# A weight half on another queue, a transposing load on ScalarE's queue, and a new order for the first projections

## The chip, the cores and the metric

The kernel runs on one core of one Trainium2 chip. Such a core has five engines that run their own instruction streams: TensorE (PE, the matmuls, with a separate stream of weight loads called PEld in the profile), VectorE (DVE), ScalarE (ACT), GpSimd (POOL) and SyncE (SP). SP does no arithmetic; here it issues DMAs, and ACT issues a few as well. Each engine takes its instructions in the order in which they stand, and an instruction that has to wait holds up everything behind it on the same engine. The engines meet through semaphores: an instruction waits until a counter has reached a value, and DMAs raise such counters when they have landed.

The metric is the device time of one execution in microseconds (us). The kernel before has a median of 178.42 us over three runs (178.19 to 178.46). The profile below is of one further execution that took 178.12 us; its span, from the first to the last instruction, is 176.3 us, so 1.8 us lie around the span.

## The reference

The input `x` has 2048 tokens of 512 numbers in bf16. Two branches are computed from it and mixed token by token with a gate:

```
g = sigmoid((x * gate_w).sum(-1))
# A: linear attention, 32 heads of 16
q, k, v = split(x @ wqkv)
phi(t)  = where(t > 0, t + 1, exp(t)) + 1e-6
kv = phi(k)^T v   per head;   z = sum over tokens of phi(k)
a  = (phi(q) kv) / (phi(q) . z + 1e-6)  @ wo
# B: a gated feed-forward block with F = 1376
b  = (silu(x @ w1) * (x @ w3)) @ w2
out = g * a + (1 - g) * b
```

## The kernel before, in words

The tokens lie in 16 tiles of 128, and four tiles make one of four blocks of 512. The width 512 is cut into `KC` = 4 chunks of 128, so that one projection of a tile (128 tokens by 512 columns) is four matmuls that add up in one PSUM buffer, one for each chunk `kc`.

**What the projections read.** `k` of tile t (`emit_k_mm`, line 195) takes as its stationary side the transposed tokens `xT[:, kc, tile t]` and as its moving side `wk_sb[:, kc, :]`. So chunk `kc` of tile t needs the transposed tile t and chunk `kc` of `wk`. `wk_sb` comes in two halves: chunks 0 and 1 (line 84) and chunks 2 and 3 (line 85), both issued by ACT.

**How `xT` is filled.** Tile 0 is loaded plainly into `x_sb` (line 83) and transposed on TensorE by `emit_xT(0)` (lines 180 to 192), whose two copies out of PSUM run on DVE (chunks 0 and 1) and ACT (chunks 2 and 3). All other tiles come by DMAs that transpose on their way: tile 1 and then tiles 2 and 3 in one load of 256 tokens (lines 88 and 89), and then blocks 1, 2 and 3 with 512 tokens each (line 92). Between these stand the plain loads of `x_sb` (line 97). After them come `wq`, the remainder columns `wr`, `wv`, `w1`, `w3`, `wo` and `w2` (lines 98 to 112). All of it stands on SP's queue in that order; before the change no transposing load stands on another queue.

**The beginning on TensorE.** `emit_warm` (line 163) first runs matmuls over constants into a PSUM buffer that nobody reads: 20 that use 32 columns of the array each (line 168), one of 128 by 128 (line 172), then come the four transposes of tile 0, three more warm matmuls, and the four `k` projections of block 0 in the order of the tiles, each with its four chunks (lines 418 to 421). After each projection `emit_k_phi` applies phi (line 145 Exp on ACT, lines 147 and 150 on DVE) and adds the result into `pks` on POOL (lines 203 and 205). From tile 4 on, `k` projections alternate with `emit_xp(u)` (line 215), which multiplies `x_sb` of a tile with phi(k) of the same tile; it needs phi of tile u. The order on TensorE is the order of the source, since PE is under a manual schedule throughout; ACT and DVE are ordered by a scheduler except where a `manual_schedule` names them.

**The later stages.** After the 16 `k` projections come `q` of block 0, the remainder columns, the small product `kvT` (lines 463 to 470), the first gate projection `gate0`, of which `emit_gate_tiled` (line 326) runs 16 matmuls that use 32 columns each, the product `W_ps` (line 487), and then the feed-forward block with the outputs, block by block.

The semaphore waits are placed by the framework that builds the program; the source does not name them.

Of the kernel before, what the change touches and what calls it, by code (L numbers as in the profile page):

```python
# [11 lines left out]
ENG = mybir.EngineType  # L12
# [5 lines left out]
def kernel(  # L18
# [12 lines left out]
    nc = tc.nc  # L31
    P = nc.NUM_PARTITIONS

    Bb, S, D = A_x.shape
# [3 lines left out]
    KC = D // P  # L38
    NT = S // P
    TB = 512  # L40
    NTB = S // TB
    TPB = TB // P
    FC = F // P
    FR = F - FC * P
    FM = FC * P
    NR = 2 * FR + 1
# [5 lines left out]
    x2d = A_x.flatten_outer_dims()  # L52
# [13 lines left out]
    xT = consts.tile([P, KC, S], BF16, name="xT")  # L66
    wk_sb = consts.tile([P, KC, D], BF16, name="wk_sb")
# [4 lines left out]
    wr_sb = consts.tile([P, KC, 2 * P], BF16, name="wr_sb")  # L72
# [4 lines left out]
    wqkv_r = A_wqkv.rearrange("(kc d) n -> d kc n", d=P)  # L77
# [2 lines left out]
    x_r = x2d.rearrange("(t p) d -> p t d", p=P)  # L80
    dq = nc.sync
    TF = 1
    dq.dma_start(out=x_sb[:, 0, :], in_=x2d[0:P, :])
    nc.scalar.dma_start(out=wk_sb[:, 0:2, :], in_=wqkv_r[:, 0:2, D : 2 * D])  # L84
    nc.scalar.dma_start(out=wk_sb[:, 2:4, :], in_=wqkv_r[:, 2:4, D : 2 * D])
    pre = consts.tile([1, 1], FP32, name="pre")
    nc.scalar.activation(out=pre[:], in_=nc.const_aps.tensor(0.0, [1, 1], FP32), func=ACT.Exp)
    for tsl in (slice(P, 2 * P), slice(2 * P, TB)):
        dq.dma_start(out=xT[:, :, tsl], in_=x2d[tsl, :], transpose=True)
    x_cut = [TF, TPB + 2, 3 * TPB, NT]  # L90
    for tb in range(1, NTB):
        dq.dma_start(
            out=xT[:, :, tb * TB : (tb + 1) * TB], in_=x2d[tb * TB : (tb + 1) * TB, :],
            transpose=True,
# [4 lines left out]
    dq.dma_start(out=wr_sb[:, :, 0:FR], in_=w1_r[:, :, FM:F])  # L99
    dq.dma_start(out=wr_sb[:, :, FR : 2 * FR], in_=w3_r[:, :, FM:F])  # L100
    with nc.allow_non_contiguous_dma(reason="one gate weight per partition and chunk"):
        dq.dma_start(
            out=wr_sb[:, :, 2 * FR : NR], in_=gate_w.rearrange("(kc d o) -> d kc o", d=P, o=1)
        )
    dq.dma_start(out=wv_sb[:], in_=wqkv_r[:, :, 2 * D : 3 * D])
    dq.dma_start(out=w1_sb[:], in_=w1_r[:, :, 0:FM])
    for fsl in (slice(0, FM // 2), slice(FM // 2, FM)):
# [12 lines left out]
        out=bm, in_=bm, pattern=[[-Dh, HPC], [0, Dh]], compare_op=ALU.is_ge, fill=0.0,  # L120
# [3 lines left out]
        out=bm, in_=bm, pattern=[[Dh, HPC], [0, Dh]], compare_op=ALU.is_ge, fill=0.0,  # L124
# [18 lines left out]
    def phi(dst, ps):  # L143
        e = work.tile([P, D], BF16, tag="phi_e", name="phi_e")
        e_ins = nc.scalar.activation(out=e[:], in_=ps, func=ACT.Exp)  # L145
        em = work.tile([P, D], BF16, tag="phi_m", name="phi_m")
        nc.vector.tensor_scalar(  # L147
            out=em[:], in0=e[:], scalar1=1.0, scalar2=1e-6, op0=ALU.min, op1=ALU.add
        )
        nc.vector.scalar_tensor_tensor(  # L150
            out=dst, in0=ps, scalar=0.0, in1=em[:], op0=ALU.max, op1=ALU.add
        )
        return e_ins
# [9 lines left out]
    def emit_warm(tiled, whole, tag="XP3"):  # L163
        warm = psX.tile([P, TB], FP32, tag=tag, name="warm")
        for n in tiled:
            for i in range(NG):
                gsl = slice(i * G, (i + 1) * G)
                nc.tensor.matmul(
                    warm[gsl, 0:n], lhsT=warm_l[:, gsl], rhs=warm_r[:, 0:n], start=True, stop=True
                )  # L170
        for n in whole:
            nc.tensor.matmul(
                warm[:, 0:n], lhsT=warm_l, rhs=warm_r[:, 0:n], start=True, stop=True
            )

    emit_warm((TB, TB, TB, TB, TB), (P,))

    st = {}

    def emit_xT(t):  # L180
        for h in range(2):
            xTp = psX.tile([P, 2, P], BF16, tag=f"XP{(2 * t + h) % 4}", name="xTp")
            for j in range(2):
                kc = 2 * h + j
                nc.tensor.transpose(
                    out=xTp[:, j, :], in_=x_sb[:, t, kc * P : (kc + 1) * P], identity=ident[:]
                )
            xT_t = xT[:, 2 * h : 2 * h + 2, t * P : (t + 1) * P]
            if h == 0:
                nc.vector.tensor_copy(out=xT_t, in_=xTp[:])  # L190
            else:
                nc.scalar.activation(out=xT_t, in_=xTp[:], func=ACT.Copy)

    def emit_k_mm(k_ps, t, kc):
        nc.tensor.matmul(  # L195
            k_ps[:], lhsT=xT[:, kc, t * P : (t + 1) * P], rhs=wk_sb[:, kc, :],
            start=(kc == 0), stop=(kc == KC - 1),
        )

    def emit_k_phi(k_ps, t):  # L200
        e_ins = phi(pk_sb[:, t, :], k_ps[:])
        if t == 0:
            nc.gpsimd.tensor_copy(pks[:], pk_sb[:, t, :])
        else:
            nc.gpsimd.tensor_add(pks[:], pks[:], pk_sb[:, t, :])  # L205
# [117 lines left out]
            )  # L323
        st[tb, "pqT"] = pqT

    def emit_gate_tiled(gate_ps):
        for kc in range(KC):
            for i in range(NG):
                gsl = slice(i * G, (i + 1) * G)
                nc.tensor.matmul(  # L330
                    gate_ps[gsl, :], lhsT=w1_sb[:, kc, gsl], rhs=xT[:, kc, 0:TB],
                    start=(kc == 0), stop=(kc == KC - 1),
                )
# [79 lines left out]


    k0 = [psM.tile([P, D], FP32, tag="mm", name=f"k0_{t}") for t in range(TPB)]
    emit_xT(0)
    emit_warm((), (P, P, P))
    for t in range(TPB):
        for kc in range(KC):
            emit_k_mm(k0[t], t, kc)  # L420
        emit_k_phi(k0[t], t)

# [11 lines left out]
    with tc.manual_schedule(engines={ENG.DVE}):  # L434
        Q = 32
        NB = D // Q
        zt = consts.tile([P, NB, Q], FP32, name="zt")
        nc.vector.transpose(out=zt[:].rearrange("p b f -> p (b f)"), in_=pks[:])
        w = Q // 2
        while w >= 1:  # L440
            nc.gpsimd.tensor_add(zt[:, :, 0:w], zt[:, :, 0:w], zt[:, :, w : 2 * w])
            w //= 2
        zq = zt[:, :, 0]
        z_up = consts.tile([P // 2, NB], FP32, name="z_up")
        z_h = consts.tile([P // 2, NB], FP32, name="z_h")
        z_hi = consts.tile([Q, NB], FP32, name="z_hi")
        z_col = consts.tile([P, NB], FP32, name="z_col")
        nc.gpsimd.tensor_copy(z_up[:], zq[P // 2 : P, :])
        nc.gpsimd.tensor_add(z_h[:], zq[0 : P // 2, :], z_up[:])
        nc.gpsimd.tensor_copy(z_hi[:], z_h[Q : 2 * Q, :])  # L450
        for b in range(P // Q):
            nc.gpsimd.tensor_add(z_col[b * Q : (b + 1) * Q, :], z_h[0:Q, :], z_hi[:])
        for dc in range(KC):
            if dc % 2 == 0:
                nc.scalar.activation(out=XP_sb[:, dc, :], in_=XP_ps[dc][:], func=ACT.Copy)
            else:
                nc.vector.tensor_copy(out=XP_sb[:, dc, :], in_=XP_ps[dc][:])

        emit_q(0, TPB - 1, psM, "mm")
        rem0 = [emit_rem_mm(0, half, psM, "mm") for half in range(2)]  # L460
        kvT_ps = psX.tile([P, KC, G], FP32, tag="XP0", name="kvT_ps")
        gate0 = psM.tile([P, TB], FP32, tag="mm", name="gate0")
        for c in range(KC):
            for dc in range(KC):
                for i in range(NG):
                    bsl = slice(c * P + i * G, c * P + (i + 1) * G)
                    nc.tensor.matmul(  # L467
                        kvT_ps[i * G : (i + 1) * G, c, :], lhsT=wv_sb[:, dc, bsl],
                        rhs=XP_sb[:, dc, bsl], start=(dc == 0), stop=(dc == KC - 1),
                    )  # L470
        nc.vector.tensor_tensor(
            out=kvT_sb[:], in0=kvT_ps[:],
            in1=diagmask[:, None, :].to_broadcast([P, KC, G]), op=ALU.mult,
        )
        for half in range(2):
            emit_rem_h(0, half, *rem0[half])
        nc.vector.transpose(
            out=z_sb[:].rearrange("p (b f) -> p b f", f=Q),
            in_=z_col[:, :, None].to_broadcast([P, NB, Q]),
        )  # L480

        emit_gate_tiled(gate0)
        W_ps = [psX.tile([P, D], FP32, tag=f"XP{i}", name=f"W_ps{i}") for i in range(NG)]
        for i in range(NG):
            gsl = slice(i * G, (i + 1) * G)
            for c in range(KC):
                nc.tensor.matmul(  # L487
                    W_ps[i][c * G : (c + 1) * G, :], lhsT=kvT_sb[gsl, c, :],
                    rhs=wo_sb[gsl, c, :], start=True, stop=True,
                )  # L490

        emit_omg(0)
        emit_ffn(0, 0, gate=gate0)
# [72 lines left out]
```

## Time and profile before

| what | us |
|---|---|
| median of three runs | 178.42 |
| the profiled execution | 178.12 |
| its span | 176.3 |
| TensorE busy in the span | 172.7 |
| VectorE busy | 119.9 |
| ScalarE busy | 64.5 |
| GpSimd busy | 66.9 |

The granted TensorE clock is 1.000 over the whole span. In the profile a row of the timeline gives the start and the length in us, the engine, the line, the operation, what is written from what, and how many instructions are merged in the row; in brackets stands how long the engine was idle ahead of it and what ended that. `SPq` and `ACTq` are instructions by which SP and ACT issue DMAs; the time from that issue to the landing of the data stands in the list of DMA issues. `L195` is line 195. The records of successive matmuls overlap, so that the chain of waits, which counts from start to start, is the better measure of the pace.

### The profile page before, as it was taken

What the parts mean: (1) busy time and instruction counts of PE and PEld (TensorE: products, weight loads), DVE (VectorE), ACT (ScalarE), POOL (GpSimd) and SP (SyncE); (2) the same over time, 40 slices, a digit from 0 to 9 for tenths busy, and PEclk for the clock granted to TensorE, in tenths of its full rate; (3) what the DMA queues carried; (4) which work ended last, traced back from release to release, by engine and by line L of the source; (5) the groups of instructions that cost most, each with busy time, mean ns of one, the idle gap of its engine ahead of it and who ended that gap; (6) DMA issues with size and microseconds to landing.
All of it is one profiled execution on the core that took longest, in us unless ns stands there. A gap on an engine that the chain in (4) does not pass through costs nothing.

```text
span 176.3 us, 2655 instructions
## 1 busy us (share of the span) xinstructions
PE 172.7 (98%) x966; PEld 82.6 (47%) x966; DVE 119.9 (68%) x204; ACT 64.5 (37%) x121; POOL 66.9 (38%) x100
## 2 busy tenths in 40 slices
PE   8999999999999999999999999999999999999994
PEld 3344444464445454444454544444545444444463
DVE  0588778898999637597875466977854669776000
ACT  4442224475424333324243333233434323331222
POOL 7298555779109423282003232820032329100000
DMA  5999999911002311124000101240002022300002
GB/s 174 236 271 281 262 386 363 348 45 26 9 4 60 67 37 37 37 63 89 0 0 7 58 20 47 59 82 0 6 7 67 7 66 54 66 4 0 30 30 60
DMA packets 30524, 15.27 MB, mean 87 GB/s; under 512 B 21456, under 2 KB 30000, under 8 KB 30512
## 3 DMA queue, kind: packets, MB, share of 16 engines
q1 hardware_dynamic: 29824, 14.54, 30.3%
q10 hardware_dynamic: 688, 0.57, 1.0%
q8 instruction: 7, 0.11, 0.3%
q14 instruction: 5, 0.04, 0.1%
HBM read 8.42 MB, written 2.10 MB: 60 GB/s over the span
## 4 chain that ended last, share of the span: by engine, by line
PE 96%; DMA 2%; ACTq 0%; DVE 0%; issue 0%
PE up_ps L353 20%; PE o_ps L395 20%; PE gate_ps L345 19%; PE o_ps L386 8%; PE q_ps L228 8%; PE XP L215 8%; PE k_ps L195 6%; PE r_ps L251 3%; DMA wk_sb<-in_A_wqkv_dram 2%; PE o_ps L390 2%; PE k L195 2%; PE gate L330 0%; PE kvT_ps L467 0%; ACTq L84 0%; PE W_ps L487 0%; DVE o_last L404 0%
## 5 line engine op out<-in xcount | busy, mean ns | idle before, releaser
L353 PE MATMUL up_ps<-xT,w_sb 128*128 128x512 bf16 x160 | 41.1, 379 | 0.0
L345 PE MATMUL gate_ps<-xT,w_sb 128*128 128x512 bf16 x156 | 40.0, 379 | 0.0
L236 POOL TENSOR_TENSOR qz<-pq,z_sb 128x512 f32<-128x512 bf16 x16 | 18.5, 1164 | 53.5 <-DVE pq L150 53.5
L358 ACT ACTIVATE th<-gate_ps 128x512 bf16<-128x512 f32 x39 | 23.3, 597 | 39.8 <-PE gate_ps L345 38.3
L395 PE MATMUL o_ps<-w_sb,hT 128*128 128x512 bf16 (+3 forms) x180 | 37.5, 355 | 0.0
L360 DVE SCALAR_TENSOR_TENSOR gs<-th,gate_ps 128x512 bf16<-128x512 bf16 x39 | 26.6, 683 | 5.6 <-ACT th L358 5.3
L365 DVE TENSOR_TENSOR hT<-up_ps,gs 128x512 bf16<-128x512 f32 x40 | 27.5, 690 | 3.7 <-PE gate_ps L345 0.5
L147 DVE TENSOR_SCALAR phi_m<-phi_e 128x512 bf16<-128x512 bf16 x32 | 16.2, 507 | 19.6 <-ACT phi_e L145 19.5
L311 POOL TENSOR_TENSOR pqn<-pq,rden 128x256 bf16<-128x256 bf16 x32 | 19.0, 625 | 16.5 <-DVE rden L302 15.1
L395 PEld LDWEIGHTS <-hT 128*128 128x128 bf16 x180 | 16.9, 98 | 17.8
L353 PEld LDWEIGHTS <-w_sb 128*128 128x128 bf16 x160 | 15.6, 98 | 18.9 <-issue 0.2
L345 PEld LDWEIGHTS <-w_sb 128*128 128x128 bf16 x156 | 15.3, 98 | 18.4
L400 ACT ACTIVATE o_out<-o_ps,omg 128x512 bf16<-128x512 f32 x15 | 10.3, 687 | 28.7 <-PE o_ps L395 28.7
L205 POOL TENSOR_TENSOR pks<-pks,pk_sb 128x512 f32<-128x512 f32 x15 | 17.4, 1158 | 8.1 <-DVE pk_sb L150 7.6
L386 PE MATMUL o_ps<-W_sb,pqT 128*128 128x512 bf16 (+3 forms) x72 | 16.8, 355 | 0.0
L228 PE MATMUL q_ps<-wq_sb,xT 128*128 128x512 bf16 x64 | 16.4, 379 | 0.0
L239 DVE TENSOR_REDUCE den<-qz 128x32 f32<-128x512 f32 x16 | 11.0, 685 | 7.9 <-POOL qz L236 7.8
L215 PE MATMUL XP<-pk_sb,x_sb 128*128 128x512 bf16 x64 | 15.9, 379 | 0.0
L145 ACT ACTIVATE phi_e<-k_ps 128x512 bf16<-128x512 f32 x12 | 7.2, 597 | 14.4 <-PE k_ps L195 10.4
L145 ACT ACTIVATE phi_e<-q_ps 128x512 bf16<-128x512 f32 x16 | 9.6, 597 | 7.8 <-PE q_ps L228 7.8
L195 PE MATMUL k_ps<-wk_sb,xT 128*128 128x512 bf16 x48 | 12.0, 379 | 0.0
L150 DVE SCALAR_TENSOR_TENSOR pq<-q_ps,phi_m 128x512 bf16<-128x512 f32 x16 | 11.1, 691 | 0.5
(68 smaller groups left out, 119.4 us busy)
## 6 DMA issues: line engine op xcount, KB each, us to landing
w_sb<-in_B_w_dram SPq DMA_DIRECT2D x2, 1280.0 KB, 9.7
out_dram<-o_out SPq DMA_DIRECT2D x15, 128.0 KB, 1.7
w_sb<-in_B_w_dram SPq DMA_DIRECT2D x2, 640.0 KB, 8.3
x_sb<-in_A_x_dram SPq DMA_DIRECT2D x1, 768.0 KB, 5.2
x_sb<-in_A_x_dram SPq DMA_DIRECT2D x1, 640.0 KB, 4.4
wk_sb<-in_A_wqkv_dram ACTq DMA_DIRECT2D x2, 256.0 KB, 3.3
x_sb<-in_A_x_dram SPq DMA_DIRECT2D x1, 512.0 KB, 4.8
wq_sb<-in_A_wqkv_dram SPq DMA_DIRECT2D x1, 512.0 KB, 5.7
```

What stands on the lines that cost most here:

```text
L195: nc.tensor.matmul(k_ps[:], lhsT=xT[:, kc, t * P : (t + 1) * P], rhs=wk_sb[:, kc, :], start=(kc == 0), stop=(kc == KC - 1),)
L215: nc.tensor.matmul(XP_ps[dc][:], lhsT=x_sb[:, t, dc * P : (dc + 1) * P], rhs=pk_sb[:, t, :], start=(t == 0), stop=(t == NT - 1),)
L228: nc.tensor.matmul(q_ps[:], lhsT=xT[:, kc, ts_tok], rhs=wq_sb[:, kc, :], start=(kc == 0), stop=(kc == KC - 1),)
L236: nc.gpsimd.tensor_tensor(out=qz[:], in0=st[tb, "pq"][:, tt, :], in1=z_sb[:], op=ALU.mult)
L311: nc.gpsimd.tensor_tensor(out=pqn[:].rearrange("p (i c e) -> p c i e", i=NG, c=KC)[:, :, :, dsl], in0=st[tb, "pq"][:, tt, :].rearrange("p ...
L345: nc.tensor.matmul(gate_ps[:], lhsT=w1_sb[:, kc, fsl], rhs=xT[:, kc, tok_sl], start=(kc == 0), stop=(kc == KC - 1),)
L353: nc.tensor.matmul(up_ps[:], lhsT=w3_sb[:, kc, fsl], rhs=xT[:, kc, tok_sl], start=(kc == 0), stop=(kc == KC - 1),)
L358: nc.scalar.activation(out=th[:], in_=gate_ps[:], func=ACT.Tanh, scale=0.5)
L360: nc.vector.scalar_tensor_tensor(out=gs[:], in0=th[:], scalar=1.0, in1=gate_ps[:], op0=ALU.add, op1=ALU.mult)
L365: nc.vector.tensor_tensor(out=st[tb, "hT"][:, fc, :], in0=up_ps[:], in1=gs[:], op=ALU.mult)
L386: nc.tensor.matmul(o_ps[:], lhsT=st[tb, "pqT"][:, c, tsl], rhs=W_sb[:, c, a:b], start=(c == 0), stop=False,)
L395: nc.tensor.matmul(o_ps[:], lhsT=st[tb, "hT"][:, fc, tsl], rhs=w2_sb[:, fc, a:b], start=False, stop=(fc == FC - 1),)
```

## The change

Five things are done:

- The second half of `wk` is issued by SP, between the transposing load of tile 1 and the next one, instead of by ACT at the beginning.
- The load of tiles 2 and 3 becomes two. Tile 2 stays on SP's queue. Tile 3 is issued by ACT, in a manual schedule of ACT that holds `emit_xT(0)` and this load, so that it stands behind ACT's copy of tile 0's transposes and ahead of phi.
- Tiles 0 and 1 take `wk`'s first half first: the order of (chunk, tile) is (0,0), (1,0), (0,1), (1,1), (2,0), (3,0), then phi of tile 0, then chunks 2 and 3 of tile 1, then tiles 2 and 3 as before.
- One warm matmul of 128 by 128 ahead of the transposes is left out.
- Of the 16 matmuls of `gate0`, the four of chunk 0 move between the second and the third column group of `kvT`.

The naming of `gate_r` ahead of its use changes nothing.

```diff
@@ -80,13 +80,16 @@
     dq = nc.sync
     TF = 1
+    gate_r = gate_w.rearrange("(kc d o) -> d kc o", d=P, o=1)
     dq.dma_start(out=x_sb[:, 0, :], in_=x2d[0:P, :])
     nc.scalar.dma_start(out=wk_sb[:, 0:2, :], in_=wqkv_r[:, 0:2, D : 2 * D])
-    nc.scalar.dma_start(out=wk_sb[:, 2:4, :], in_=wqkv_r[:, 2:4, D : 2 * D])
     pre = consts.tile([1, 1], FP32, name="pre")
     nc.scalar.activation(out=pre[:], in_=nc.const_aps.tensor(0.0, [1, 1], FP32), func=ACT.Exp)
-    for tsl in (slice(P, 2 * P), slice(2 * P, TB)):
+    for t in range(TF, TPB - 1):
+        tsl = slice(t * P, (t + 1) * P)
         dq.dma_start(out=xT[:, :, tsl], in_=x2d[tsl, :], transpose=True)
+        if t == TF:
+            dq.dma_start(out=wk_sb[:, 2:4, :], in_=wqkv_r[:, 2:4, D : 2 * D])
...
@@ -173,7 +174,7 @@
-    emit_warm((TB, TB, TB, TB, TB), (P,))
+    emit_warm((TB, TB, TB, TB, TB), ())
...
-    def emit_gate_tiled(gate_ps):
-        for kc in range(KC):
+    def emit_gate_tiled(gate_ps, lo, hi):
+        for kc in range(lo, hi):
...
@@ -413,10 +414,16 @@
     k0 = [psM.tile([P, D], FP32, tag="mm", name=f"k0_{t}") for t in range(TPB)]
-    emit_xT(0)
+    with tc.manual_schedule(engines={ENG.Activation}):
+        emit_xT(0)
+        t3sl = slice(3 * P, TB)
+        nc.scalar.dma_start(out=xT[:, :, t3sl], in_=x2d[t3sl, :], transpose=True)
     emit_warm((), (P, P, P))
-    for t in range(TPB):
-        for kc in range(KC):
+    for kc, t in ((0, 0), (1, 0), (0, 1), (1, 1), (2, 0), (3, 0)):
+        emit_k_mm(k0[t], t, kc)
+    emit_k_phi(k0[0], 0)
+    for t in range(1, TPB):
+        for kc in range(2 if t == 1 else 0, KC):
             emit_k_mm(k0[t], t, kc)
         emit_k_phi(k0[t], t)
...
@@ -461,6 +468,8 @@
         for c in range(KC):
+            if c == KC // 2:
+                emit_gate_tiled(gate0, 0, 1)
             for dc in range(KC):
...
-        emit_gate_tiled(gate0)
+        emit_gate_tiled(gate0, 1, KC)
```

More of the change, by code (lines that the diff above doesn't have):

```diff
@@ L101 @@
     with nc.allow_non_contiguous_dma(reason="one gate weight per partition and chunk"):
-        dq.dma_start(
-            out=wr_sb[:, :, 2 * FR : NR], in_=gate_w.rearrange("(kc d o) -> d kc o", d=P, o=1)
-        )
+        dq.dma_start(out=wr_sb[:, :, 2 * FR : NR], in_=gate_r)
     dq.dma_start(out=wv_sb[:], in_=wqkv_r[:, :, 2 * D : 3 * D])
```

## The prediction

> **What bounds the kernel now.** I read the page's chain of waits first, then the chain in order of time, then the timeline of the first nine microseconds, and last the list of DMA issues for narrow stretches.
>
> The page's chain of what ended last has one line by engine:
>
> ```profile
> PE 96%; DMA 2%; ACTq 0%; DVE 0%; issue 0%
> ```
>
> TensorE carries the span. In order of time (start, length, what) the beginning reads:
>
> ```profile
> 0.80 0.46 ACTq L84
> 1.26 0.03 issue
> 1.29 3.70 DMA wk_sb<-in_A_wqkv_dram
> 4.99 0.04 issue
> 5.03 3.34 PE k L195 x14
> 8.38 0.86 PE XP L215 x4
> 9.24 2.59 PE k_ps L195 x12
> ```
>
> The reader is to see two things. Up to 5.03 us the chain waits for `wk`'s second half; from there to the last matmul TensorE does not stop. So time can be won only ahead of 5 us, and any new stop of TensorE goes into the time in full. The pace of the full clock is also here: 12 matmuls in 2.59 us, 0.216 us each. The timeline (start, length, engine, line, what) shows how the pieces of the beginning stand:
>
> ```profile
> 0.84 2.33 PE L168 MATMUL warm<-const-bfloat16-1.0 128*32 128x512 bf16 x20 [0.84 <-PEq L550]
> ...
> 1.26 2.62 SPq L89 DMA_TRANSPOSE xT<-in_A_x_dram  x2
> 1.29 0.49 ACTq L85 DMA_DIRECT2D wk_sb<-in_A_wqkv_dram  x1
> ...
> 3.85 0.38 ACT L192 ACTIVATE xT<-xTp 128x256 bf16<-128x256 bf16 x1 [0.54 <-PE xTp L185]
> 3.93 2.17 SPq L92 DMA_TRANSPOSE xT<-in_A_x_dram  x1
> 3.98 0.13 PEld L195 LDWEIGHTS <-xT 128*128 128x128 bf16 x2
> 3.99 0.86 PE L195 MATMUL k<-wk_sb,xT 128*128 128x512 bf16 x2
> ...
> 5.03 3.34 PE L195 MATMUL k<-wk_sb,xT 128*128 128x512 bf16 x14 [0.18 <-DMA wk_sb<-in_A_wqkv_dram]
> ...
> 5.41 0.59 PEld L195 LDWEIGHTS <-xT 128*128 128x128 bf16 x4 [0.28 <-DMA xT<-in_A_x_dram]
> ...
> 6.47 1.41 PEld L195 LDWEIGHTS <-xT 128*128 128x128 bf16 x8 [0.48 <-DMA xT<-in_A_x_dram]
> ...
> 6.77 3.53 SPq L92 DMA_TRANSPOSE xT<-in_A_x_dram  x1
> ```
>
> TensorE waits 0.18 us for `wk`; tile 1 arrives just in time (5.41), and so do tiles 2 and 3 (6.47). The four matmuls of tile 3 are the last of the fourteen; they start 0.86 us ahead of 8.38, at 7.52 us. The list of DMA issues for stretches around one issue gives the time from issue to landing, first around 1.5 us (tile 1), then around 6.7 us (block 2):
>
> ```profile
> xT<-in_A_x_dram SPq DMA_TRANSPOSE x1, 4.1
> ...
> xT<-in_A_x_dram SPq DMA_TRANSPOSE x1, 5.7
> ```
>
> So tile 1 lands at 1.26 + 4.1 = 5.4 us, and block 2 at 6.77 + 5.7 = 12.5 us, five microseconds after TensorE wants tile 3.
>
> **The change part by part.** *Tile 3 on ACT's queue* is the term that decides. In the changed program as it is built, ACT's load of tile 3 stands behind waits for five DMA counters: those of the plain tile 0, of the transposing loads of tile 1, tile 2 and block 1, and of the transposing load of block 2. By these waits the framework keeps the transposing loads of two queues apart; all three block loads stand ahead of tile 3's in the source, and two of them in the built order. SP's load of block 3 in its turn waits for tile 3's counter. TensorE's first weight load of tile 3 waits for that counter too. Nothing of this exists before.
>
> When ACT is released: SP issues, in the new order, tile 0, tile 1, `wk`'s half (0.49, its row on ACT), tile 2 (1.28; the merged row of two is 2.62 for 128 and 256 tokens, so the size hardly matters here), block 1, the plain five tiles, block 2. Against before one plain issue is added, 0.49 and a gap of 0.04: block 2 is issued at 6.77 + 0.53 = 7.30 and lands, with the same 5.7, at 13.0. It could be earlier, since 128 KB less stand ahead of it in a stretch that moved 250 to 300 GB/s: 0.5 us off, 12.0 without the later issue. Or later: a plain load now breaks the run of transposes once more. I take 12.9, ends 12.0 and 13.4.
>
> How long tile 3 takes: the nearest row is tile 1's load, the same 128 tokens from the same tensor beside 640 KB of plain loads: 4.1. At 13 us it runs beside the plain load of six tiles, 768 KB. The transposing loads of `pqT`, equal in size but out of SBUF and with a quiet queue, have a median of 2.4. Block 2 itself, four times the size in a full queue, has 5.7. I take 3.6, nearest to tile 1 and a little shorter since tile 1's also held the start of everything; ends 2.4 and 5.7. Landing: 12.9 + 3.6 = 16.5 us.
>
> TensorE is in order: behind tile 3's weight load stand `XP` of tile 0, `k` of tile 4 and all that follows. It starts tile 3 at 16.5 instead of 7.52: **+9.0 us**.
>
> *The clock after the stop.* The first two `k` matmuls took 0.86 us, 0.43 each, against 0.216 later. TensorE ran at half pace from 0.84 to 4.85 us, 4.0 us of work that would have been 2.0: the ramp costs 2.0 us once. Between tile 2's end (issued at 3.1, 4.0 to its landing as the median of the two loads before, 0.86 of matmuls: 7.9) and 16.5 it stands still for 8.6 us, longer than that whole ramp. The trace of before has no such stop in the middle, so what comes after one is bounded by 0 and by a full second ramp, 2.0. I take **+2.0**, because the only rows that follow idleness are the slow ones.
>
> [...]
>
> *ACT held up.* ACT waits from 4.23 (the end of its copy at 3.85 + 0.38) to 12.9, and behind that wait stand the Exps of tiles 0 to 2, for which DVE, POOL and later `XP` wait. ACT is free again after an issue of 1.28 at 14.2; Exp 0.60, then 0.29 and 0.69 on DVE give phi of tile 0 at about 15.8, ahead of `XP`, which can't start before tile 3's four matmuls, 16.5 plus 0.86 or more. Tiles 1 and 2 follow at about one microsecond each, and free the PSUM buffers for tiles 5 and 6 in time, as TensorE at half pace takes 1.7 us for each group of four. Cost nothing; the cover is TensorE's own late start.
>
> *SP held up.* Block 3's issue moves from 10.97 to 16.5, and all weights behind it by as much, 5.5 us; TensorE's need for each moves by 11. No weight made TensorE wait before, so none does now. Nothing.
>
> *`wk`'s half and the new order.* The half is issued at about 2.6 instead of 1.29 and lands, with 2.2 (tile 0's plain load) to 3.7 (its own row), at 4.8 to 6.3. The first four matmuls need tile 1, which landed at 5.4, and are through by 5.8. So the 0.18 of waiting may go, or become a wait of up to 0.5. TensorE ends in front of tile 3 anyway and waits there for 8 us: in the sum 0.
>
> *The warm matmul left out.* It ran at 3.10, while tile 0 landed at 0.81 + 2.2 = 3.01; tile 0's transposes may start some 0.1 earlier. Also swallowed: 0.
>
> *`gate0`'s four matmuls among `kvT`'s.* The same 16 and 64 matmuls in another order. `kvT`'s last ends a quarter of the gate's 0.88 later, 0.22, and DVE's masked copy (0.29) with it; `W_ps` waits for that copy; in between TensorE now has 12 gate matmuls, three quarters of 0.88, 0.66 us, over 0.29 and DVE's gap of 0.1. Cost 0; with that cover gone 0.3. In the built order one small Exp on ACT falls behind the gate's Tanh (0.58), so DVE's first feed-forward step comes about 0.5 later. Its second product ends at 43.55, and TensorE wants that buffer at 44.46, so 0.9 of slack holds it.
>
> **The sum.** 9.0 + 2.0 = 11.0 us on the profiled 178.12: 189.1. The median stands 0.3 above the profiled execution, so 189.4 us is the forecast.
>
> [...]
>
> **The rivals.**
>
> 1. *The clock does not fall.* Only the stop of 9.0 counts: 187.4 us. Speaks for it: the granted clock in the profile is 1.000 throughout, even in the slow rows, so it does not show this state. Against: those slow rows themselves.
> 2. *Tile 3 lands later still*, as a load beside 768 KB in a full queue: with block 2's 5.7 it lands at 18.6, 11.1 after 7.52, plus 2.0: 191.5 us. For it: landings grow from 4.1 to 5.7 and 8.0 for blocks 2 and 3. Against: those are four times the size.
> 3. *The stop is not there*, the other side: if tile 3 landed by 7.5, TensorE would lose nothing and keep what is won ahead, the 0.18 wait for `wk` and 0.1 of the warm matmul: 178.1 us. It decides at a landing of 7.5, for which ACT would have to be released by 3.9 (3.6 earlier), ahead of the end of its own copy at 4.23. Only if the waits stood for loads that are done early could this be.
> 4. *The stop is short*, because only tiles 1 and 2 need be waited for: ACT released near 7.0, landing at 10.6, a stop of 3.1, shorter than the ramp and taken without one: 181.5 us. Against it stand the counters of blocks 1 and 2.
>
> **How the numbers follow.** I give the forecast 0.64, rival 1 0.13, rival 2 0.17, rival 3 0.03, rival 4 0.03. Within 0.2% of before, which is about what a measurement of this kernel can tell from no change, lies rival 3's 178.1: 0.02 for the same and, as it might win a little more, 0.01 for faster. Slower is the rest, 0.97. The bounds together: 12.0 + 2.4 = 14.4 gives +6.9, with the ramp 187.3, without it 185.3; 13.4 + 5.7 = 19.1 gives +11.6 + 2.0, 192.0. The range takes in most of that, 186.5 to 191.8 us; the low end leaves out rival 1 with the earliest landing, and the two rivals below it.
>
> **What would show it.** In the profile of the changed kernel the wait list of ACT should have a wait of about 8.7 us for the DMA of `xT` at line 420; TensorE should be idle about 8.6 us in one piece before the last four `k` matmuls of block 0, released by `xT`; the matmuls behind it should go at 0.43 each for some 4 us; the last three slices of weights should land without a wait of TensorE; and nothing in the span behind some 21 us should be longer than before. Wrong would be: a stop that ends before 14 us or after 19, matmuls at 0.216 right behind it, or a second wait of TensorE, for phi or for block 3.

## The result, and the profile after

The changed kernel takes 190.91 us (median of six runs, 190.35 to 191.82) against 178.45 us before (six runs, 178.19 to 179.05): 1.070 times as long, 95% interval 1.068 to 1.073. The forecast was 189.4 us with a range of 186.5 to 191.8. The profiled execution took 190.56 us with a span of 188.8 us, 12.5 us more than the span before.

Two lines of the page of the changed kernel, the chain's shares by engine and the granted TensorE clock in 40 slices of the span, in tenths:

```profile
PE 89%; DMA 5%; SPq 3%; issue 1%; DVE 0%; ACTq 0%
...
PEclk9975699999999999999999999999999999999999
```

TensorE's share has fallen from 96% to 89%, that of DMAs has grown from 2% to 5%, and SP's issues have come in with 3%. The page of before has no line for the clock; now there is one, and it has a dip in slices 3 to 5, about 9 to 24 us. The chain of waits in order of time (start, length, what), from 7 us on:

```profile
7.36 6.41 DMA xT<-in_A_x_dram
13.77 0.02 issue
13.79 0.04 ACTq L420
13.82 0.04 issue
13.86 3.39 DMA xT<-in_A_x_dram
17.25 0.05 issue
17.30 1.89 PE k L196 x4
19.19 1.71 PE XP L216 x4
20.89 0.85 PE k_ps L196 x2
21.75 0.21 issue
21.95 2.11 PE k_ps L196 x9
24.06 0.86 PE XP L216 x4
...
185.95 0.28 DVE o_last L405
```

The same chain before has the second group of `XP` and the last eviction here:

```profile
11.83 0.86 PE XP L215 x4
...
173.76 0.28 DVE o_last L404
```

This is the whole story in one column. Block 2's transposing load is issued at 7.36 and lands 6.41 later; that releases line 420 on ACT; tile 3's load takes 3.39; then TensorE starts tile 3 at 17.30. Before, it started tile 3 at 7.52, so it is 9.78 us late. From there to the second group of `XP` it now needs 24.06 - 17.30 = 6.76 us, where it needed 11.83 - 7.52 = 4.31: another 2.45. From 24 us on the two chains run in step: the last matmuls' eviction on DVE starts at 185.95 instead of 173.76, 12.19 later. The remaining 0.3 lie in the final stores.

The timeline (start, length, engine, line, what, and in brackets the idle time ahead and its end) shows who waits:

```profile
6.26 1.89 PE L196 MATMUL k<-wk_sb,xT 128*128 128x512 bf16 x8 [0.77 <-DMA wk_sb<-in_A_wqkv_dram]
...
7.36 4.39 SPq L95 DMA_TRANSPOSE xT<-in_A_x_dram  x1
11.79 0.58 SPq L100 DMA_DIRECT2D x_sb<-in_A_x_dram  x1
13.86 1.27 ACTq L420 DMA_TRANSPOSE xT<-in_A_x_dram  x1
15.18 1.57 ACT L146 ACTIVATE phi_e<-k 128x512 bf16<-128x512 f32 x3 [11.05 <-issue]
...
17.27 2.00 SPq L95 DMA_TRANSPOSE xT<-in_A_x_dram  x1
...
17.30 1.89 PE L196 MATMUL k<-wk_sb,xT 128*128 128x512 bf16 x4 [9.15 <-DMA xT<-in_A_x_dram]
```

ACT computes nothing from 4.13 to 15.18, TensorE nothing for 9.15 us, and SP issues block 3 only at 17.27, when tile 3 has landed. The idle time of the first Exp is put down to "issue" and not to a DMA: the load's own wait for other loads does not show as a wait of ACT in this view; it is seen from the start of the row of line 420.

The windows of the same kernel give, for each stretch, its length, the busy time of PE, PEld, DVE, ACT and POOL, then the granted clock, the share of the DMA engines and their GB/s:

```profile
8.00:12.00 4.00, 0.15 (x1) 0.00 (x0) 0.00 (x0) 0.00 (x0) 0.00 (x0) 0.96 0.98 241
12.00:16.00 4.00, 0.00 (x0) 0.00 (x0) 0.19 (x1) 0.82 (x2) 0.00 (x0) 0.50 0.96 263
16.00:18.00 2.00, 0.70 (x2) 0.28 (x3) 1.90 (x6) 0.76 (x2) 0.70 (x2) 0.50 0.37 85
...
21.00:22.00 1.00, 0.79 (x3) 0.35 (x3) 0.17 (x1) 0.00 (x0) 0.69 (x1) 0.53 0.85 247
22.00:24.00 2.00, 2.00 (x10) 0.93 (x10) 0.97 (x3) 1.19 (x2) 0.47 (x1) 1.00 1.07 353
```

A mean of 0.96 over 8 to 12 us means, with the 1.00 and 0.50 of the stretches on either side, that the clock went from 1.00 to 0.50 at about 11.7, some 3.5 us after TensorE had stopped. It came back at 21.9 (0.53 over 21 to 22), 4.6 us after TensorE had started again.

### The profile page after: what moved, and what is told of

It is laid out like the page before. It is cut to its first block, busy times and chain, and to the rows that moved or that the text cites. A ratio compares the mean times of both kernels' runs of the same rounds, so it can differ in the third digit from the quotient of the medians.

```text
span 188.8 us, 2641 instructions
## 1 busy us (share of the span) xinstructions
PE 174.0 (92%) x949; PEld 83.0 (44%) x965; DVE 118.1 (63%) x204; ACT 64.1 (34%) x121; POOL 66.8 (35%) x100
## 4 chain that ended last, share of the span: by engine, by line
PE 89%; DMA 5%; SPq 3%; issue 1%; DVE 0%; ACTq 0%
PE up_ps L354 18%; PE o_ps L396 18%; PE gate_ps L346 18%; PE XP L216 8%; PE o_ps L387 7%; PE q_ps L229 7%; PE k_ps L196 6%; DMA xT<-in_A_x_dram 5%; PE r_ps L252 3%; PE o_ps L391 2%; SPq L90 1%; SPq L95 1%; PE k L196 1%; PE gate L331 0%; SPq L100 0%
## 5 line engine op out<-in xcount | busy, mean ns | idle before, releaser
L148 DVE TENSOR_SCALAR phi_m<-phi_e 128x512 bf16<-128x512 bf16 x32 | 14.3, 448 | 33.5 <-ACT phi_e L146 33.5
L396 PEld LDWEIGHTS <-hT 128*128 128x128 bf16 x180 | 16.8, 98 | 17.8
L354 PEld LDWEIGHTS <-w_sb 128*128 128x128 bf16 x160 | 15.6, 98 | 18.9 <-issue 0.2
L216 PE MATMUL XP<-pk_sb,x_sb 128*128 128x512 bf16 x62 | 16.6, 395 | 0.1
L196 PEld LDWEIGHTS <-xT 128*128 128x128 bf16 x64 | 6.5, 103 | 19.4 <-DMA xT<-in_A_x_dram 10.4
L196 PE MATMUL k<-wk_sb,xT 128*128 128x512 bf16 x16 | 5.2, 466 | 10.0 <-DMA xT<-in_A_x_dram 9.2
L146 ACT ACTIVATE phi_e<-k_ps 128x512 bf16<-128x512 f32 x12 | 7.2, 597 | 15.8 <-PE k_ps L196 14.7
```

Source lines behind the costliest of these rows:

```text
L196: nc.tensor.matmul(k_ps[:], lhsT=xT[:, kc, t * P : (t + 1) * P], rhs=wk_sb[:, kc, :], start=(kc == 0), stop=(kc == KC - 1),)
L216: nc.tensor.matmul(XP_ps[dc][:], lhsT=x_sb[:, t, dc * P : (dc + 1) * P], rhs=pk_sb[:, t, :], start=(t == 0), stop=(t == NT - 1),)
L354: nc.tensor.matmul(up_ps[:], lhsT=w3_sb[:, kc, fsl], rhs=xT[:, kc, tok_sl], start=(kc == 0), stop=(kc == KC - 1),)
L396: nc.tensor.matmul(o_ps[:], lhsT=st[tb, "hT"][:, fc, tsl], rhs=w2_sb[:, fc, a:b], start=False, stop=(fc == FC - 1),)
```

## The experiments

The theory was: the loss is the wait of ACT's load for block 2's load, and then the second ramp of the clock. Against it stood: that other parts of the change carry a part of the loss, that any load on ACT's queue would do this, and that the slow stretch behind the stop comes from late phi and not from the clock.

**Tile 3 on ACT's queue, and nothing else.** The kernel before with this edit:

```diff
-    for tsl in (slice(P, 2 * P), slice(2 * P, TB)):
+    for tsl in (slice(P, 2 * P), slice(2 * P, 3 * P)):
...
-    emit_xT(0)
+    with tc.manual_schedule(engines={ENG.Activation}):
+        emit_xT(0)
+        t3sl = slice(3 * P, TB)
+        nc.scalar.dma_start(out=xT[:, :, t3sl], in_=x2d[t3sl, :], transpose=True)
```

> The kernel before with one edit: tile 3's transposing load is taken out of the load of tiles 2 and 3 and issued by ScalarE behind its copy of tile 0's transposes; wk, the order of the projections, the warm matmul and the gate stay as before. Theory (ScalarE's load waits for block 2's load, and nothing else in the change matters): block 2 lands at about 12.5 us, tile 3 3.4 later at 15.9, TensorE's last four k matmuls of block 0 start 8.4 later than before, plus 2.4 for the second ramp of the clock: 189.2 us, 188 to 190.5. Rival (the stop needs the later half of wk or the new order): 178.4 to 180 us.

Measured: 189.08 us against 178.65 us, ratio 1.059 (1.055 to 1.064). Two rows of its timeline:

```profile
13.19 1.28 ACTq L419 DMA_TRANSPOSE xT<-in_A_x_dram  x1
...
16.34 1.89 PE L195 MATMUL k<-wk_sb,xT 128*128 128x512 bf16 x4 [8.61 <-DMA xT<-in_A_x_dram]
```

The one edit brings 10.4 of the 12.5 us. Tile 3 is 16.34 - 7.52 = 8.8 us late, and the ramp, measured as above up to the second group of `XP` (at 22.32), is 1.7. The other 2 us of the changed kernel are a start of tile 3 that is 0.96 later (block 2 is issued at 7.36 instead of 6.62, and tile 3's own load takes 3.39 instead of 3.10) and a ramp that is 0.8 longer.

**Tile 3 back on the sync queue, the rest of the change kept.**

```diff
-    for t in range(TF, TPB - 1):
+    for t in range(TF, TPB):
...
-    with tc.manual_schedule(engines={ENG.Activation}):
-        emit_xT(0)
-        t3sl = slice(3 * P, TB)
-        nc.scalar.dma_start(out=xT[:, :, t3sl], in_=x2d[t3sl, :], transpose=True)
+    emit_xT(0)
```

> The changed kernel, but tile 3's transposing load stands on the sync queue right behind tile 2's; the rest of the change stays. Theory (all of the large loss is tile 3 on ScalarE's queue; the rest costs a little since wk's second half lands at 6.2 instead of 5.0 us and each further transposing issue takes 1.28): tile 3 lands at about 8.3, its four matmuls end at about 9.2 instead of 8.4: 179.2 us, 178.7 to 179.8. Rival (the moved half of wk and the new order carry part of the loss): 181 us or more. Second rival (the rest of the change by itself is a gain): 178.2 us or less.

Measured: 179.63 us against 178.41, ratio 1.0065 (1.0045 to 1.0085). What TensorE waits for in it (us in total, times, longest):

```profile
PE k_ps L196 <- DMA xT<-in_A_x_dram: 0.7, 1, 0.7
PE k L196 <- DMA wk_sb<-in_A_wqkv_dram: 0.4, 1, 0.4
PE XP L216 <- DMA x_sb<-in_A_x_dram: 0.3, 1, 0.3
```

So the rest is a loss too, of 1.2 us, and a small one: `wk`'s half comes late, and since tiles 2 and 3 now cost two issues of some 1.2 us each, block 1 and the plain tiles behind it come late as well.

**`wk`'s half back on ACT's queue as well.** The run before, and:

```diff
     nc.scalar.dma_start(out=wk_sb[:, 0:2, :], in_=wqkv_r[:, 0:2, D : 2 * D])
+    nc.scalar.dma_start(out=wk_sb[:, 2:4, :], in_=wqkv_r[:, 2:4, D : 2 * D])
...
-        if t == TF:
-            dq.dma_start(out=wk_sb[:, 2:4, :], in_=wqkv_r[:, 2:4, D : 2 * D])
```

> The changed kernel with tile 3 on the sync queue (as in the run before it) and wk's second half back on ScalarE's queue at the beginning; the new order of the projections stays. Theory: wk's half lands at 5.0 again and TensorE does not wait for it; tile 3 lands at about 7.7 and block 1 some 1.3 later than before: 178.7 us, 178.4 to 179.0, about 0.5 less than with wk's half on the sync queue. Rival (the place of wk's half makes no difference): the same time as the run with wk's half on the sync queue, within 0.2.

Measured: 179.06 us against 178.41, ratio 1.0045 (1.0021 to 1.0069), a little above the range expected; two of its twelve runs took 180.5 and 180.9 us, the others at most 179.6. Against the run before it, on the same chip, it is 0.57 us less by the medians, as the theory had it, but the two intervals overlap, so this difference is likely rather than settled. What is left, about 0.65, is the split of the load and the order of the projections: TensorE waits 0.6 for tile 1, because the new order wants tile 1 ahead of `wk`'s second half, and 0.5 for block 1.

**The gate and the warm matmul alone**, on the kernel before:

```diff
-    emit_warm((TB, TB, TB, TB, TB), (P,))
+    emit_warm((TB, TB, TB, TB, TB), ())
...
         for c in range(KC):
+            if c == KC // 2:
+                emit_gate_tiled(gate0, 0, 1)
...
-        emit_gate_tiled(gate0)
+        emit_gate_tiled(gate0, 1, KC)
```

> The kernel before with only the two small edits: the one warm matmul of 128 by 128 ahead of the transposes left out, and the gate's four matmuls of chunk 0 moved between kvT's. Theory: both lie beside other work, 178.4 us, within 0.2 of the kernel before. Rival (the later kvT makes TensorE wait for its masked copy, or the Exp that now stands behind the gate's Tanh delays VectorE): 0.3 to 0.6 us slower.

Measured: 178.51 us against 178.41, ratio 1.0004 (0.9991 to 1.0017). Nothing, as expected.

**The same load in plain form.** Is it ACT's queue, or the transposing form on it? The changed kernel with:

```diff
...
-        t3sl = slice(3 * P, TB)
-        nc.scalar.dma_start(out=xT[:, :, t3sl], in_=x2d[t3sl, :], transpose=True)
+        x3_sb = consts.tile([P, D], BF16, name="x3_sb")
+        nc.scalar.dma_start(out=x3_sb[:], in_=x2d[3 * P : TB, :])
...
     for t in range(1, TPB):
+        if t == 3:
+            emit_xT(3, x3_sb)
```

> The changed kernel, but ScalarE's load of tile 3 is a plain one into a buffer of its own, and TensorE transposes it as it does tile 0 (four transposes, a copy on VectorE and one on ScalarE). Theory (the wait belongs to the transposing form on a second queue): no wait for the blocks, the load lands at 6.3 to 7.8 us, and tile 3's matmuls end some 1 to 1.5 us later than before: 179.8 us, 179.0 to 180.5. Rival (any load on ScalarE's queue at this place brings the stop): 188 us or more.

Measured: 180.23 us against 178.41, ratio 1.0092 (1.0071 to 1.0113). Its timeline has the load at ACT's place in the order, right behind the copy:

```profile
4.12 0.38 ACT L193 ACTIVATE xT<-xTp 128x256 bf16<-128x256 bf16 x1 [1.33 <-PE xTp L186]
4.12 0.35 ACTq L420 DMA_DIRECT2D x_sb<-in_A_x_dram  x1
```

It is issued at 4.12 instead of 13.86, so not every load at this place on ACT's queue brings the stop. The wait goes with the transposing form.

**Warm matmuls in the stop.** The changed kernel with TensorE kept at work:

```diff
     for t in range(1, TPB):
+        if t == 3:
+            emit_warm((), (TB,) * 41)
```

> The changed kernel with 41 warm matmuls of 512 columns (8.9 us at 0.216 each) in TensorE's order between tile 2's and tile 3's k matmuls, into a buffer that nobody reads. Theory (some 2.4 us of the loss are the clock's second ramp): tile 3 still starts at about 17.3 us, the matmuls behind it go at 0.216, and the time falls to about 188.5 us, 188.0 to 189.0. Rival (the slow stretch behind the stop comes from late phi, PSUM buffers or loads): it stays at 190.4 to 191.4 us.

Measured: 188.17 us against 178.65, ratio 1.0547 (1.0523 to 1.0572). In its timeline the warm matmuls fill the stop, and tile 3 starts nearly when it did:

```profile
7.90 9.13 PE L173 MATMUL warm<-const-bfloat16-1.0 128*128 128x512 bf16 x40
...
13.78 1.26 ACTq L420 DMA_TRANSPOSE xT<-in_A_x_dram  x1
...
17.06 1.04 PE L196 MATMUL k<-wk_sb,xT 128*128 128x512 bf16 x4
...
21.39 1.03 PE L216 MATMUL XP<-pk_sb,x_sb 128*128 128x512 bf16 x4
```

The four matmuls of tile 3 take a record of 1.04 us instead of 1.89, and the granted clock is 1.00 throughout. From tile 3 to the second group of `XP` it is 21.39 - 17.06 = 4.33 us, where the changed kernel needs 6.76 and the kernel before 4.31. Phi and the loads are as late as in the changed kernel (the first Exp at 15.09 instead of 15.18, ACT's load at 13.78 instead of 13.86), and the time falls by 2.7 us, of which 0.24, by the profiled executions, are tile 3's earlier start. So the slow stretch behind the stop is the clock.

**Fewer loads ahead of tile 3.** The changed kernel, with the loads of blocks 2 and 3 moved behind tile 3's in the source and tied there by two writes of one element into their targets:

```diff
...
         nc.scalar.dma_start(out=xT[:, :, t3sl], in_=x2d[t3sl, :], transpose=True)
+        zero = nc.const_aps.tensor(0.0, [1, 1], FP32)
+        for c0 in (2 * TB, 3 * TB):
+            nc.scalar.activation(out=xT[0:1, 0, c0 : c0 + 1], in_=zero, func=ACT.Copy)
+
+    for tb in range(2, NTB):
...
```

> The changed kernel, but the transposing loads of blocks 2 and 3 are held behind tile 3's load by two one-element writes of ScalarE into their targets, which stand right behind that load. ScalarE then waits for tiles 1 and 2 and block 1 alone. Theory (the stop is as long as the last transposing load that stands ahead takes to land, plus 3.4): block 1 lands at about 8.7 us, tile 3 at 12.1, so the stop shrinks from 9.2 to about 4 us; 183.0 us without a second ramp, 185.4 with a full one. Rival (a transposing load on ScalarE's queue is slow in itself, whatever stands ahead): 189 to 191 us.

Measured: 189.62 us against 178.65, ratio 1.0626 (1.0604 to 1.0647). The time lies in the range of the rival, but neither account holds: tile 3 lands at 15.9 and not at 12.1, and the two runs that follow show that the queue is not slow in itself. Rows of its timeline, and then of its list of DMA issues (KB, us to landing):

```profile
7.08 1.11 SPq L413 DMA_DIRECT2D x_sb<-in_A_x_dram  x2
8.62 1.32 ACTq L402 DMA_TRANSPOSE xT<-in_A_x_dram  x1
...
15.90 1.89 PE L178 MATMUL k<-wk_sb,xT 128*128 128x512 bf16 x4 [8.25 <-DMA xT<-in_A_x_dram]
```

```profile
x_sb<-in_A_x_dram SPq DMA_DIRECT2D x1, 512.0 KB, 8.0
...
xT<-in_A_x_dram ACTq DMA_TRANSPOSE x1, 7.2
```

ACT is released at 8.6, as the theory said. But the load then takes 7.2 us instead of 3.4. In this kernel SP did not wait: the scheduler drew the plain loads of 768 and 512 KB forward to 7.08, ahead of tile 3, and the second of them, issued at about 7.6, lands at 15.6, just ahead of tile 3 at 15.9. So 3.4 us is not what such a load takes in every place. Two further runs took up the new reading, that what is in the way is whatever was issued ahead, on either queue. One puts all later loads behind tile 3, the plain ones too:

```diff
...
         nc.scalar.dma_start(out=xT[:, :, t3sl], in_=x2d[t3sl, :], transpose=True)
+        zero = nc.const_aps.tensor(0.0, [1, 1], FP32)
+        nc.scalar.activation(out=xT[0:1, 0, 2 * TB : 2 * TB + 1], in_=zero, func=ACT.Copy)
+
+    with tc.manual_schedule(engines={ENG.SP}):
+        for tb in range(2, NTB):
...
```

> The run that held blocks 2 and 3 behind tile 3 again, but now the plain loads of the later tiles and of all weights are held there too: one element of block 2's target is written by ScalarE behind tile 3's load, and the sync queue keeps its source order from there. Ahead of tile 3 stand tiles 1 and 2, block 1 and one plain load of 640 KB. New theory (tile 3 lands some 0.4 us after the last load that was issued ahead of it on either queue, transposing or plain): ScalarE is released at about 8.6 us, the plain load lands at 11.6, tile 3 at about 12.0, the stop is 4 to 4.4 us: 185.3 us with a full second ramp, 183.0 without one. Rival (a transposing load on ScalarE's queue is slow in itself, 7.2 us as in the run before): tile 3 lands at about 15.9 again, 189 to 190 us.

Measured: 186.01 us against 178.70, ratio 1.0408 (1.0390 to 1.0427).

```profile
9.35 1.28 ACTq L402 DMA_TRANSPOSE xT<-in_A_x_dram  x1
...
12.75 1.89 PE L178 MATMUL k<-wk_sb,xT 128*128 128x512 bf16 x4 [4.65 <-DMA xT<-in_A_x_dram]
```

Block 1 lands at 9.25 and not at 8.7, the plain load of 640 KB at 6.63 + 5.4 = 12.0 and not at 11.6, and tile 3 at 12.7. The load takes 3.4 again. The stop is 4.65 us, and the ramp that follows 2.85: the clock had fallen at about 11.4, before TensorE started again, and came back at 18.2. A stop half as long (4.65 us against 9.15) came with no smaller ramp (2.85 against 2.45).

The other leaves ACT's wait for block 2 as it is and only keeps the 768 KB and what follows them behind tile 3:

```diff
...
         nc.scalar.dma_start(out=xT[:, :, t3sl], in_=x2d[t3sl, :], transpose=True)
+        zero = nc.const_aps.tensor(0.0, [1, 1], FP32)
+        nc.scalar.activation(out=x_sb[0:1, x_cut[1], 0:1], in_=zero, func=ACT.Copy)
...
```

> The changed kernel with only the plain load of 768 KB (six tiles) and what follows it held behind tile 3's load, by a one-element write of ScalarE into that load's target; ScalarE still waits for block 2. New theory (the plain load ahead is in tile 3's way): ScalarE is released at about 13.8 us as before, tile 3 lands 2.4 to 2.7 us later instead of 3.4, at about 16.4: 190.1 us, 189.6 to 190.5. Rival (3.4 us is what such a load takes): 17.2 us again, 190.9 us, 190.4 to 191.5.

Measured: 189.66 us against 178.70, ratio 1.0596 (1.0551 to 1.0640).

```profile
14.02 1.27 ACTq L403 DMA_TRANSPOSE xT<-in_A_x_dram  x1
...
16.77 1.89 PE L179 MATMUL k<-wk_sb,xT 128*128 128x512 bf16 x4 [8.83 <-DMA xT<-in_A_x_dram]
```

With no plain load ahead of it any more the load lands after 2.7 us. One and the same load thus took 2.7, 3.4 and 7.2 us, by what plain load was ahead of it on the other queue. In the five kernels with plain loads ahead (the changed kernel: 11.79 + 5.0 = 16.8 and 17.25; with the warm matmuls: 11.69 + 4.9 = 16.6 and 17.0; tile 3 alone: 10.98 + 4.8 = 15.8 and 16.3; the two runs ahead of this one: 15.6 and 15.9, 12.0 and 12.7) tile 3 lands 0.3 to 0.7 us behind the last of them.

The DMA view also counts the packets of each queue: `q1` is SP's, `q10` is ACT's (tile 3's 128 KB are 544 packets of it in the changed kernel). In the run with the 7.2 us, for 10 to 13.2 us (packets, MB, share of the 16 DMA engines):

```profile
q1 hardware_dynamic: 1146, 1.14, 105.4%
q10 hardware_dynamic: 42, 0.01, 1.5%
```

Tile 3's load was issued at 8.62 there. From 9 to 10 us only SP's queue moves packets (367), and of ACT's 42 have moved by 13.2 us. In the changed kernel SP's queue alone moves from 13.86 to 15.5 (482 packets), and tile 3's 544 all fall between 15.5 and 17. So tile 3's data went nearly behind the plain data that were issued ahead of it, on another queue. In these two traces the packets of the two queues mix only towards the end of the plain load: 241 of SP's beside the 544 between 15.5 and 17 us in the changed kernel, 220 beside 178 over 13 to 14 us in the run with the 7.2 us. What sets this order the runs do not tell.

## Why the prediction was right

- *The wait of tile 3's load* was the deciding step, and it held. It was to be +9.0 us and is +9.78. Of its terms the issue of block 2 was right (7.30 foretold, 7.36 measured). The time to its landing was the mis-sized one: 5.7 was carried over from before, and it took 6.4 (6.5 with tile 3 alone), so ACT was released at 13.86 and not at 12.9. The DMAs moved 215 and 225 GB/s over 6 to 8 and 8 to 10 us, where they had moved 253 and 297 before; why is open. Tile 3's own 3.6 was 3.4, which is in part luck: it was taken from tile 1's 4.1 as the nearest in size and form, and with size and form unchanged the same load took 2.7 to 7.2, by what stood ahead.
- *The clock after the stop* held in kind. The ramp was 2.45 us, and the warm matmuls took all but 0.02 of it away, where the sum had 2.0, the author's estimate from the slow rows at the start. The prediction also took 2.0, the ramp at the start, as the most that it could be, and that was wrong: 1.7 in the kernel with tile 3 alone, 2.45 in the changed kernel, 2.85 in the run with the stop of 4.65 us.
- *Rival 1, the clock does not fall*, is refuted, and so is what was said for it: that the granted clock in the profile would not show this state. It shows 0.50 here. At the start of the kernel it reads 1.00 although the matmuls are as slow (0.43 us each); why is not shown.
- *Rival 2, tile 3 lands later still*, had 191.5 us, and the measured 190.91 is nearer to that than to the forecast of 189.4. Its mechanism is not what happened, for it had 5.7 us for tile 3's load, which took 3.4; block 2's landing and the ramp made up the difference. *Rivals 3 and 4*, no stop and a short one, fell with ACT's release at 13.86.
- *ACT held up* cost nothing: phi of tile 0 was there at 16.14 + 0.69 = 16.83, a microsecond later than foretold, and `XP` came at 19.19. *SP held up* cost nothing: block 3 was issued at 17.27, and no load made TensorE wait afterwards.
- *`wk`'s half and the new order* were put at 0 in the sum with a wait of up to 0.5. The wait was 0.77, because tile 1 landed at 4.7 and not at 5.4, but it lies ahead of a stop that tile 3's landing ends, as said. Without the stop it is a loss: with the split load it costs 1.2 us.
- *The warm matmul and the gate's four matmuls* at 0: 1.0004 in the run with them alone.
- *The sum* had 11.0 in place of 12.5 in the spans: 0.8 from the stop, 0.45 from the ramp, and 0.3 in the final stores, which no step had.
- *What would show it*: the stop in one piece (9.15 us), the matmuls at 0.43 behind it for 4.6 us and a rest without a new wait for loads are there; only the slow pace reached to 21.9 instead of 21 us. The wait list does not name ACT's wait for the DMA; it goes as "issue", and that part of the forecast was wrong about the view.

## What to carry to other kernels

A transposing load on a second queue waited in every kernel here for the transposing loads that the schedule had put ahead of it on the first (it was issued at 8.6 to 14.0 us, the plain load in its place at 4.12; in the changed kernel at 13.86, with the last of them landed at 13.77), and the order in the source did not show which these were: look at the waits of the program as it is built before a load is moved to an idle queue. Put such a load on the queue that has the others, or make it plain and transpose on TensorE; with the rest of the change these cost 1.2 and 1.8 us here instead of 12.5. And count a stop of TensorE of 4.65 us or more, the shortest one measured here, as the stop plus 1.7 to 2.9 us of ramp.

## What the runs showed of the hardware that was not expected

The time that the clock stayed low had two lengths. In the five kernels with a stop, the clock fell 3.0 to 4.8 us after TensorE had stopped. For four of them the windows also hold its return, which came 3.1 to 5.45 us after TensorE had started again. The time from the fall to the return was 6.84 us in two (12.56 to 19.40 with tile 3 alone, 11.36 to 18.20 with all later loads behind tile 3) and 10.24 us in the other two (11.69 to 21.93 in the changed kernel, 11.72 to 21.96 with the 768 KB held back). These ends are worked out from mean clocks: over windows of 0.04 us in the changed kernel, of 2 us in the others. The mean clock over the whole span also has two levels in all executions of these kernels: 0.973, and 0.981 or 0.982. With tile 3 alone it is 0.981 in the executions of 188.21 and 188.63 us and 0.973 in those of 189.53 and 190.04. Why there are two lengths is not shown.

The cost of the ramp goes with the return. In these four it was half the time from the restart to the return plus some 0.1 us: 1.7 for 3.1, 2.45 for 4.6, about 2.7 for 5.2 and 2.85 for 5.45. So how soon after TensorE's restart the clock returns goes with about a microsecond of time; no run set this on purpose.

A transposing load on ACT's queue took 7.2 us with 1,920 KB of plain loads issued ahead of it on SP's (640, 768 and 512), and 2.7 us where the last plain load ahead, of 640 KB, had landed at 12.0, before it was issued at 14.0. The difference of 4.5 us is more than those 2.7.
